# Frequency-domain mixing by three real products instead of four, an fp32 first transform stage, and a 512-wide weight conversion

## Chip, cores and metric

The kernel runs on one core of a Trainium2 chip, in one launch. The metric is device time in microseconds (us), the median of the runs shown. The engines are TensorE (PE, with its weight loads as PEld), VectorE (DVE), ScalarE (ACT), GpSimd (POOL) and SyncE (SP), which issues most DMAs.

## Reference

Three layers follow each other; `x` is 8 x 3072 x 256 in fp32.

```python
X = np.fft.rfft(x, axis=1); Xr, Xi = X.real, X.imag
Yr = Xr @ w_r - Xi @ w_i + b_r                 # mixing of channels, 256 x 256
Yi = Xr @ w_i + Xi @ w_r + b_i
Yr, Yi = soft_threshold(Yr, 0.01), soft_threshold(Yi, 0.01)
x = np.fft.irfft(Yr + 1j * Yi, n=3072, axis=1).reshape(24576, 256)
# soft mixture of experts over 8 batches of 3072 tokens, with an online softmax in the kernel
# gated feed-forward: rms norm, silu(xn @ w_gate) * (xn @ w_val) @ w_out    (weights in float64)
```

## The kernel before

The kernel has two phases. Phase 1 (`phase1`) does the transform, the mixing, the threshold and the sums of the softmax over tokens. Phase 2 does the feed-forward from what phase 1 kept; it takes some 1,095 us, and of it the change touches one line (917), which names three buffers.

**Precision.** TensorE multiplies either fp32 tiles or tiles of the type `fp32r`, which carry fewer bits. Where more bits are wanted from `fp32r`, a value is split into a high part (a copy rounded by ScalarE) and a low part (the rest, a subtraction), and products of parts are added up in PSUM. The trace shows an fp32 product as two records, each with its own weight load, and an `fp32r` product as one.

**Stages of phase 1, per batch.** The transform of length 3072 is split into 96 x 32.
- Stage A (`emit_A`, line 230) is a 96 x 96 product over pieces of 512 columns; a batch has 16 pieces, `g`. `split_hi` (208) and `split_lo` (224) make the two parts of the input, and line 245 does three `fp32r` matmuls. ScalarE evacuates (248), and the result goes to a DRAM buffer `bounce` and back in another order (`load_B`, 254).
- Stage B (`emit_B`, 261) is four fp32 matmuls of 128 x 128 (270). ScalarE writes the high part of the spectrum (277), VectorE the low part (280).
- Mixing (`emit_M`, 292) works on a window: a third of a batch, 512 columns, two halves `h` of the input channels and two halves `ch` of the output channels. There are 24 windows of 12 steps. Each of the four outputs (real or imaginary, `ch`) takes three steps of four `fp32r` matmuls (313): 48 a window. Then ScalarE (320) and VectorE (323) apply the threshold, both from PSUM.
- `emit_T` (353) transposes the result, `emit_L` (365) makes logits' spectra, and `chain` (384) is the list of the softmax work of one batch, by step.

**Order.** The schedule is by hand. The loop at line 693 runs the 288 steps `u`; a step emits for each engine, in program order: what `post` put off to this step (evacuations one step after their matmuls, VectorE's part two steps after), then chain work, `emit_M`, stage A, transposes, stage B. Each engine works its own list in order. PSUM banks: one for A, two for B, two for M, one for T.

**Weight conversion.** `converter` (100) turns the float64 weights into fp32 by integer operations on VectorE, 256 values wide: 36 jobs, nine or ten VectorE instructions each (132 to 150). It is a generator; line 743 lets it go on by one piece in those steps for which `load`, a running estimate of VectorE's work (tables `fixed` and `chained`, `pace` a step), is below `room`.

**Memory and the end of phase 1.** Pools are closed when their stage is done, and `Mid.open(n)` puts buffers of 1 MB in their place and loads expert weights into them (line 794, on SP): 5 buffers with 4 loads at step 252, 1 at step 279, 6 after the last step, 4 later. Behind these loads on SP stand the softmax result of the last batch (480), the four loads of `cs` (871) and what phase 2 starts with.

Of the kernel before, what the change touches and what calls it, by code (L numbers as in the profile page):

```python
# [99 lines left out]
def converter(tc, st, w_gate, w_val, w_out, wgv_d, wo_d):  # L100
# [4 lines left out]
    for i, w in enumerate((w_gate, w_val)):  # L105
        v = w.bitcast(I32).rearrange("(k p) f -> p k f", p=128)
        for k in range(2):
            for f in range(6):
                jobs.append((v[:, k, 512 * f:512 * f + 512], wgv_d[:, k, 1536 * i + 256 * f:1536 * i + 256 * f + 256]))
    v = w_out.bitcast(I32).rearrange("(k p) c -> p k c", p=128)  # L110
    for k in range(12):
        jobs.append((v[:, k, :], (wo_d[0][:, k, :], wo_d[1][:, k, :])))

    def load(n):
        t = raw_p.tile([128, 256, 2], I32, name="cvraw")
        nc.sync.dma_start(out=t.rearrange("p n w -> p (n w)"), in_=jobs[n][0])
        return t

    def steps():
# [3 lines left out]
        for n, (_, dst) in enumerate(jobs):  # L123
# [18 lines left out]
            w = tmp_p.tile([128, 256], F32, name="cvw")  # L142
            v.scalar_tensor_tensor(out=w, in0=q, scalar=2.0 ** -44, in1=m.bitcast(F32), op0=ALU.mult, op1=ALU.add)
            v.tensor_tensor(out=w, in0=w, in1=p.bitcast(F32), op=ALU.mult)
            if isinstance(dst, tuple):
# [3 lines left out]
                nc.sync.dma_start(out=dst[0], in_=h)  # L149
                v.tensor_tensor(out=w, in0=w, in1=h, op=ALU.subtract)  # L150
# [7 lines left out]
def phase1(tc, x, w_r, w_i, b_r, b_i, phi, t_d, t_bf, t_ci, t_ai, t_af, t_id,  # L158
# [24 lines left out]
    dh = ca.tile([96, 96], F32R, name="dh")  # L183
    dl = ca.tile([96, 96], F32R, name="dl")
    wh = {k: cm.tile([128, 2, 256], F32R, name=f"wh_{k}") for k in ("r", "n", "i")}
    wl = {k: cm.tile([128, 2, 256], F32R, name=f"wl_{k}") for k in ("r", "n", "i")}
# [5 lines left out]
    xraw, xsp, asb, bounce, bin_t, xq, x0, yy, yts, lfs, mns, mix = ({} for _ in range(12))  # L192
# [15 lines left out]
    def split_hi(g, dve=False):  # L208
        b, i, h = g // 16, g // 2 % 8, g % 2
        if b == 0 and i % 2:  # L210

            if h == 0:
                xsp["t"] = xq_p.tile([128, 2, 2, 2, 512], F32R, name="xq")[0:96]
            xs = xsp["t"][:, h, 0, 0, :], xsp["t"][:, h, 1, 0, :]
        else:
            xs = xs_p.tile([96, 512], F32R, name="xhi"), xs_p.tile([96, 512], F32R, name="xlo")
        v = xraw[b, i][:, 512 * h:512 * h + 512]
        if dve:
            nc.vector.tensor_copy(out=xs[0], in_=v)
        else:  # L220
            nc.scalar.activation(out=xs[0], in_=v, func=AF.Copy)  # L221
        xsp[g] = xs + (v,)

    def split_lo(g, eng):
        hi, lo, v = xsp[g]
        eng.tensor_tensor(out=lo, in0=v, in1=hi.bitcast(F32), op=ALU.subtract)  # L226
        if g % 2 and 8 <= g // 2 < 8 * NB - 2:
            load_x(*divmod(g // 2 + 2, 8))

    def emit_A(g, ps=None):  # L230
        b, i, h = g // 16, g // 2 % 8, g % 2
        hi, lo, _ = xsp.pop(g)
# [11 lines left out]
        for k, (w, v) in enumerate(((dh, hi), (dh, lo), (dl, hi))):  # L244
            nc.tensor.matmul(out=ps, lhsT=w, rhs=v, start=(k == 0), stop=(k == 2))  # L245
# [15 lines left out]
    def emit_B(b, q, h):  # L261

        t = bin_t[b, q]
        if h == 0 and q % 2 == 0:
# [957 lines left out]
```

## Time and profile before

| | |
|---|---|
| device time, three runs | 1793.46, 1796.31, 1796.82 us; median 1796.31 us |
| profiled execution: span from first to last instruction | 1798.8 us (no other time is recorded for it) |
| TensorE busy | 1767.3 us, 98% |
| VectorE, ScalarE, GpSimd busy | 1274.8, 1084.6, 242.1 us |
| steps 0 to 287 of phase 1, about | 47 to 630 us |

The page gives the busy time of each engine and what its idle time waited for. Matmuls are pipelined, so the length of one record is more than the time between two; the distance of starts in a dense run, or the pieces of the chain, give the time that one takes. All granted clocks here are those of TensorE.

### The profile page before, as it was taken

How to read it: one execution, taken by the hardware profiler on the slowest of the kernel's cores; microseconds unless marked ns; L12 is line 12 of the kernel's file. 1: busy time of each engine (PE TensorE's matmuls, PEld its weight loads, DVE VectorE, ACT ScalarE, POOL GpSimd, SP SyncE). 2: the span in 40 equal slices, each digit the busy share in tenths (PEclk: the TensorE clock that was granted, in tenths of full speed). 3: DMA queues.
4: the chain of work that ended last, by engine and by line, in shares of the span. 5: the costliest groups of instructions: out<-in, count | busy, mean ns of one | idle time of the engine just before them, and what ended most of it. 6: DMA issues, size and time to landing. Idle time of an engine off the chain costs nothing.

```text
span 1798.8 us, 33265 instructions
## 1 busy us (share of the span) xinstructions
PE 1767.3 (98%) x12910; PEld 1536.9 (85%) x12910; DVE 1274.8 (71%) x2126; ACT 1084.6 (60%) x2185; POOL 242.1 (13%) x181
## 2 busy tenths in 40 slices
PE   7999999999999989999999999999999999999999
PEld 5777777777777746999999999999999999999998
DVE  4478787785854537777677777777777777777775
ACT  3555556565553337776676676676676676676553
POOL 2434233332321001000000000000000000000000
PEclk8999999999999999999999999999999999999999
DMA  8865654756545197223123113212213203202101
GB/s 223 238 195 170 171 166 141 202 149 180 162 115 176 39 309 202 55 60 68 33 57 62 42 43 64 53 37 59 60 33 63 66 23 73 66 18 60 31 18 36
DMA packets 157101, 180.70 MB, mean 100 GB/s; under 512 B 62304, under 2 KB 126320, under 8 KB 156944
## 3 DMA queue, kind: packets, MB, share of 16 engines
q1 hardware_dynamic: 156208, 176.62, 37.4%
q8 instruction: 102, 1.67, 0.4%
q0 software_dynamic: 624, 1.92, 0.3%
q14 instruction: 55, 0.45, 0.1%
q10 hardware_dynamic: 112, 0.04, 0.0%
HBM read 94.36 MB, written 60.56 MB: 86 GB/s over the span
## 4 chain that ended last, share of the span: by engine, by line
PE 69%; DVE 1%; DMA 1%; SPq 1%; ACT 0%; issue 0%; POOL 0%; DVEq 0%
PE pe L1108 23%; PE po L1108 22%; PE pv L1072 7%; PE pg L1070 7%; PE psM L313 4%; PE psx L847 1%; PE psB L270 1%; DMA cs<-ct_d 1%; PE psA L245 0%; PE psT L361 0%; PE psT L373 0%; PE psC L552 0%; PE psC L396 0%; PE psx L1108 0%; SPq L854 0%; DMA cq<-ex 0%
## 5 line engine op out<-in xcount | busy, mean ns | idle before, releaser
L1076 DVE TENSOR_TENSOR h<-s,pv 128x512 f32<-128x512 f32 x576 | 394.2, 684 | 262.7 <-ACT s L1074 261.0
L1074 ACT ACTIVATE s<-pg 128x512 f32<-128x512 f32 x576 | 344.4, 598 | 346.5 <-PE pg L1070 344.5
L1108 PE MATMUL pe<-wo,hh 128*128 128x256 f32 x2304 | 429.0, 279 | 0.0
L1108 PE MATMUL po<-wo,hh 128*128 128x256 f32 x2280 | 423.6, 279 | 0.0
L1108 PEld LDWEIGHTS pe<-wo,hh 128*128 128x128 f32 x2304 | 382.6, 188 | 43.2 <-DVE o L1124 2.4
L97 DVE TENSOR_TENSOR hl<-h,hh 128x512 fp32r<-128x512 f32 x572 | 407.3, 712 | 0.0
L96 ACT ACTIVATE hh<-h 128x512 fp32r<-128x512 f32 x576 | 359.8, 625 | 8.0 <-DVE h L1076 6.9
L1108 PEld LDWEIGHTS po<-wo,hh 128*128 128x128 f32 x2280 | 349.8, 188 | 3.3
L1108 PE MATMUL pe<-wo,hl 128*128 128x256 f32 x1152 | 321.1, 279 | 0.0
L1108 PE MATMUL po<-wo,hl 128*128 128x256 f32 x1140 | 317.6, 279 | 0.0
L1070 PE MATMUL pg<-cq,gst 128*128 128x512 f32 x576 | 229.4, 398 | 0.3 <-ACT s L1074 0.3
L1072 PE MATMUL pv<-cq,gst 128*128 128x512 f32 x576 | 227.8, 395 | 0.7 <-DVE h L1076 0.7
L1108 PEld LDWEIGHTS pe<-wo,hl 128*128 128x128 f32 x1152 | 216.1, 188 | 0.0
L1108 PEld LDWEIGHTS po<-wo,hl 128*128 128x128 f32 x1140 | 213.9, 188 | 0.0
L226 POOL TENSOR_TENSOR xlo<-xraw,xhi 96x512 fp32r<-96x512 f32 x107 | 142.4, 1335 | 295.2 <-ACT xhi L221 195.1
L313 PE MATMUL psM<-xq,wh_r 128*128 128x512 f32 x384 | 174.3, 454 | 2.0 <-DVE xq L280 1.1
L277 ACT ACTIVATE xq<-psB 128x512 fp32r<-128x512 f32 x96 | 57.2, 596 | 120.4 <-PE psB L270 120.4
L280 DVE TENSOR_TENSOR xq<-psB,xq 128x512 fp32r<-128x512 f32 x96 | 66.0, 688 | 87.3 <-ACT xq L277 87.2
L270 PE MATMUL psB<-bf,bin 128*128 128x128 f32 x768 | 106.1, 282 | 7.6 <-DMA bin<-bounce 7.5
L270 PEld LDWEIGHTS psB<-bf,bin 128*128 128x128 f32 x768 | 95.8, 195 | 18.9 <-issue 16.5
L1072 PEld LDWEIGHTS pv<-cq,gst 128*128 128x128 f32 x576 | 108.3, 188 | 2.2 <-DVE h L1076 1.8
L1070 PEld LDWEIGHTS pg<-cq,gst 128*128 128x128 f32 x576 | 108.1, 188 | 1.3 <-ACT s L1074 1.1
(288 smaller groups left out, 2245.8 us busy)
## 6 DMA issues: line engine op xcount, KB each, us to landing
bin<-bounce SPq DMA_DIRECT2D x192, 128.0 KB, 3.7
bounce<-asb SPq DMA_DIRECT2D x59, 384.0 KB, 3.5
xraw<-in_x_dram SPq DMA_DIRECT2D x56, 384.0 KB, 4.2
ex<-in_moe_w_dram SPq DMA_DIRECT2D x16, 1024.0 KB, 12.2
out_dram<-o SPq DMA_DIRECT2D x124, 128.0 KB, 2.2
out_dram<-o SPq DMA_DIRECT2D x132, 64.0 KB, 1.7
cs<-chi SPq DMA_DIRECT2D x56, 96.0 KB, 2.1
cs<-clo SPq DMA_DIRECT2D x56, 96.0 KB, 2.2
```

The costliest lines, as they stand in the source:

```text
L96: nc.scalar.activation(out=hi, in_=src, func=AF.Copy)
L97: (lo_eng or nc.vector).tensor_tensor(out=lo, in0=src, in1=hi.bitcast(F32), op=ALU.subtract)
L226: eng.tensor_tensor(out=lo, in0=v, in1=hi.bitcast(F32), op=ALU.subtract)
L270: nc.tensor.matmul(out=ps[:, 128 * j:128 * j + 128], lhsT=t[:, j, 128 * h:128 * h + 128], rhs=bf[:, 4 * q + j, :], start=True, stop=True)
L277: nc.scalar.activation(out=hi, in_=v, func=AF.Copy)
L280: nc.vector.tensor_tensor(out=lo, in0=v, in1=hi.bitcast(F32), op=ALU.subtract)
L313: nc.tensor.matmul(out=ps, lhsT=w, rhs=v, start=(m % 3 == 0 and n == 0), stop=(m % 3 == 2 and n == 3))
L1070: nc.tensor.matmul(out=pg, lhsT=gst[:, 128 * fb:128 * fb + 128], rhs=v, start=True, stop=True)
L1072: nc.tensor.matmul(out=pv, lhsT=gst[:, 1536 + 128 * fb:1536 + 128 * fb + 128], rhs=v, start=True, stop=True)
L1074: nc.scalar.activation(out=s, in_=pg, func=AF.Silu)
L1076: nc.vector.tensor_tensor(out=h, in0=s, in1=pv, op=ALU.mult)
L1108: nc.tensor.matmul(out=ps, lhsT=a[:, ts], rhs=w[:, fb, :], start=(fb == 0 and k == 0), stop=(fb == 11 and k == 2))
```

## The change

Mixing uses Yr = w_r (Xr + Xi) - (w_i + w_r) Xi and Yi = w_r (Xr + Xi) + (w_i - w_r) Xr. The sum Xr + Xi is made in fp32 (a copy on ScalarE, an addition on VectorE) and its product is taken in fp32; the other two are taken from split halves with three `fp32r` matmuls each. The product with w_r is copied out of PSUM by ScalarE, VectorE adds it to each of the other two, and the threshold then works in SBUF. Stage A takes its input as it is, in one fp32 matmul. The conversion is 512 wide: 18 jobs in smaller pieces. The step tables, some steps of transposes, the buffers of phase 1 and the numbers given to `Mid.open` change with it.

```diff
@@ converter: jobs of 512, 18 instead of 36
-            for f in range(6):
+            for f in range(3):
...
-    for k in range(12):
-        jobs.append((v[:, k, :], (wo_d[0][:, k, :], wo_d[1][:, k, :])))
+    for k in range(0, 12, 2):
+        jobs.append((v[:, k:k + 2, :], tuple(w[:, k:k + 2, :].rearrange("p k c -> p (k c)") for w in wo_d)))
...
@@ pools of phase 1
-    xq_p, x0_p = P(st_m, "xq", 2), P(st_m, "x0", 2)
+    xq_p, xs_p, x0_p, s_p, r_p = (P(st_m, n, k) for n, k in (("xq", 2), ("xs", 1), ("x0", 2), ("s", 2), ("r", 1)))
...
-    xr_p, xs_p, as_p = P(st_a, "xr", 2), P(st_a, "xs", 4), P(st_a, "as", 2)
+    xr_p, as_p = P(st_a, "xr", 3), P(st_a, "as", 2)
...
-    def split_hi(g, dve=False):
...
-    def split_lo(g, eng):
...
@@ emit_A
-        for k, (w, v) in enumerate(((dh, hi), (dh, lo), (dl, hi))):
-            nc.tensor.matmul(out=ps, lhsT=w, rhs=v, start=(k == 0), stop=(k == 2))
+        nc.tensor.matmul(out=ps, lhsT=dt, rhs=xraw[b, i][:, 512 * h:512 * h + 512], start=True, stop=True)
+        if h == 1:
+            xraw.pop((b, i))
+            if 8 <= g // 2 + 3 < 8 * NB and g // 2 >= 8:
+                post(lambda: load_x(*divmod(g // 2 + 3, 8)))
...
@@ emit_B
         def evac():
             nc.scalar.activation(out=hi, in_=v, func=AF.Copy)
+            nc.scalar.activation(out=xsum, in_=v[:, 2:4], func=AF.Copy)
 
         def rest():
+            nc.vector.tensor_tensor(out=xsum, in0=v[:, 0:2], in1=xsum, op=ALU.add)
             nc.vector.tensor_tensor(out=lo, in0=v, in1=hi.bitcast(F32), op=ALU.subtract)
...
@@ emit_M
-        ri, ch = UNITS[m // 3]
+        (ch, k), h = ((0, 0), (1, 0), (0, 1), (0, 2), (1, 1), (1, 2))[m // 2], m % 2
...
+        if k == 0:
+            nc.tensor.matmul(out=ps, lhsT=wf[:, h, cs], rhs=xs[b, qq][:, h], start=(h == 0), stop=(h == 1))
         else:
-            terms = [(wh[key][:, h, cs], X[:, 1, h, part]) for h in range(2) for key, part in ways]
...
+            terms = ((wh, 0), (wl, 0), (wh, 1))
+            for n, (w, p) in enumerate(terms):
+                nc.tensor.matmul(out=ps, lhsT=w[k - 1][:, h, cs], rhs=X[:, p, h, k - 1], start=(h == 0 and n == 0), stop=(h == 1 and n == 2))
+        if h == 0:
             return
         o = 1 if qq == 0 else 0
-        Y = yy[b, qq][:, ri, ch, o:]
+        if k == 0:
+            t = mix["s", ch] = s_p.tile([128, 512], F32, name="s")
+            post(lambda: nc.scalar.activation(out=t[:, o:], in_=ps[:, o:], func=AF.Copy), 1, 0)
+            return
+        ri = 2 - k
+        Y, t, late = yy[b, qq][:, ri, ch, o:], mix["s", ch], int(m == 9)
+        r = r_p.tile([128, 512], F32, name="r")
+
+        def whole():
+            nc.vector.tensor_tensor(out=Y, in0=ps[:, o:], in1=t[:, o:], op=ALU.add)
 
         def first():
-            nc.scalar.activation(out=Y, in_=ps[:, o:512], func=AF.Relu, bias=b_lo[:, ri, ch:ch + 1])
+            nc.scalar.activation(out=r[:, o:], in_=Y, func=AF.Relu, bias=b_lo[:, ri, ch:ch + 1])
 
         def end():
-            nc.vector.scalar_tensor_tensor(out=Y, in0=ps[:, o:512], scalar=b_hi[:, ri, ch:ch + 1], in1=Y, op0=ALU.add, op1=ALU.min)
+            nc.vector.scalar_tensor_tensor(out=Y, in0=Y, scalar=b_hi[:, ri, ch:ch + 1], in1=r[:, o:], op0=ALU.add, op1=ALU.min)
...
-        post(first, 1, 0)
-        post(end, 2, 0)
+        post(whole, 1 + late, 0)
+        post(first, 2 + late, 0)
+        post(end, 3 + late, 0)
...
@@ the loop of steps
-    fixed = (0.7, 0.7, 0.0, 0.0, 1.15, 0.7, 0.0, 1.4, 0.0, 0.0, 1.4, 0.0)
+    fixed = (1.8, 0.75, 0.75, 0.0, 0.0, 1.55, 0.7, 1.1, 1.45, 0.0, 1.85, 0.7)
...
-    load, room, pace = 0.0, 0.4, 1.75
+    load, room, pace = 0.0, 1.0, 1.85
...
-        if w >= 1 and m in (1, 5, 8, 10) and w <= W - 3:
+        if w >= 1 and m in (2, 5, 8, 10) and w <= W - 3:
...
-            mid.open(5, 4)
+            mid.open(4, 3)
...
-    mid.open(6)
+    mid.open(7)
```

Before the first step, `split_x` and the splits of `w_r` and `w_i` (each high and low, and the negated pair on line 620) go; instead the two matrices w_i - w_r and -(w_i + w_r) are made on VectorE and split, and w_r is loaded into `wf` as it is. A third tile of the next batch's input is loaded there, behind the third `load_B`. The 96 x 96 table is loaded into `dt` and not split.

## Rows read from the trace of the kernel before

**Rows 1.** Page, busy time, share and instructions of each engine.
```profile
PE 1767.3 (98%) x12910; PEld 1536.9 (85%) x12910; DVE 1274.8 (71%) x2126; ACT 1084.6 (60%) x2185; POOL 242.1 (13%) x181
```
**Rows 2.** Windows: length, busy us (instructions) of PE, PEld, DVE, ACT, POOL, clock, DMA share, GB/s.
```profile
0.00:47.00 47.00, 35.48 (x131) 26.01 (x132) 20.52 (x36) 18.16 (x32) 14.72 (x17) 0.85 0.82 214
...
265.00:338.00 73.00, 72.69 (x506) 55.40 (x508) 58.74 (x106) 41.29 (x75) 25.68 (x19) 1.00 0.60 168
...
47.00:630.00 583.00, 577.25 (x4084) 437.36 (x4083) 399.60 (x694) 306.33 (x555) 176.43 (x135) 0.99 0.57 162
```
**Rows 3.** Waits of PE, 120 to 484 us: total us, times, longest us (the first row).
```profile
PE psM L313 <- DVE xq L280: 1.1, 1, 1.1
```
**Rows 4.** Chain of waits, 600 to 632 us: start us, us, what.
```profile
603.21 2.80 PE psM L313 x12
...
609.65 0.86 PE psC L503 x2
610.51 0.93 PE psM L313 x4
```
**Rows 5.** Timeline of PE in the first step: start us, us, instruction.
```profile
47.69 0.39 PE L245 MATMUL psA<-xhi,dh 96*96 96x512 f32 x1
...
48.38 0.40 PE L313 MATMUL psM<-xq,wh_r 128*128 128x512 f32 x1
```
**Rows 6.** Groups by line, all of the span: VectorE and ScalarE, 512 and 256 wide.
```profile
L97 DVE TENSOR_TENSOR hl<-h,hh 128x512 fp32r<-128x512 f32 x572 | 407.3, 712 | 0.0
L1076 DVE TENSOR_TENSOR h<-s,pv 128x512 f32<-128x512 f32 x576 | 394.2, 684 | 262.7 <-ACT s L1074 261.0 <-PE pv L1072 0.6
...
L1044 ACT ACTIVATE sq<-psx 128x256 f32<-128x256 f32 x168 | 62.3, 381 | 0.0
L277 ACT ACTIVATE xq<-psB 128x512 fp32r<-128x512 f32 x96 | 57.2, 596 | 120.4 <-PE psB L270 120.4
...
L1124 DVE COPY o<-pe 128x256 f32<-128x256 f32 x96 | 36.0, 416 | 4.7 <-PE pe L1108 4.7
```
**Rows 7.** The same view: costliest and cheapest of the conversion's nine lines of 36.
```profile
L144 DVE TENSOR_TENSOR cvw<-cvw,cva 128x256 f32<-128x256 f32 x36 | 31.8, 882 | 1.2
...
L138 DVE TENSOR_SCALAR cve<-cvraw 128x256 int32<-128x256 int32 x36 | 12.4, 345 | 0.0
```
**Rows 8.** By source line, two conversion lines: ns min/median/max, first and last start.
```profile
L132 DVE TENSOR_SCALAR cva<-cvraw x36: 225/293/1234, 71.8 to 488.7; 128x256 int32<-128x256 int32 x36
...
L144 DVE TENSOR_TENSOR cvw<-cvw,cva x36: 424/427/1402, 76.7 to 497.2; 128x256 f32<-128x256 f32 x36
```
**Rows 9.** Groups by line, GpSimd, 47 to 630 us.
```profile
L226 POOL TENSOR_TENSOR xlo<-xraw,xhi 96x512 fp32r<-96x512 f32 x105 | 139.9, 1336 | 281.1 <-ACT xhi L221 181.0 <-PE psA L245 52.9 <-ACT yy L320 22.4
L464 POOL TENSOR_TENSOR ch<-ch,mc 96x1024 f32<-96x1024 f32 x7 | 13.7, 1957 | 7.0 <-ACT xq L277 7.0
```
**Rows 10.** Timeline of all engines before the first step.
```profile
6.00 0.44 PE L245 MATMUL psA<-xhi,dh 96*96 96x512 f32 x1 [0.49 <-DVE xhi L219]
...
22.41 0.47 PE L245 MATMUL psB<-xq,dh 96*96 96x512 f32 x1 [0.97 <-POOL xq L226]
...
32.21 0.42 DVE L620 TENSOR_SCALAR wl_n<-wl_i 128x512 fp32r<-128x512 f32 x1
...
32.86 3.42 PE L270 MATMUL psB<-bf,bin 128*128 128x128 f32 x16 [3.00 <-DMA bin<-bounce]
```
**Rows 11.** Timeline of SP's DMA issues, end of phase 1.
```profile
611.63 45.74 SPq L794 DMA_DIRECT2D ex<-in_moe_w_dram  x12
657.46 3.39 SPq L480 DMA_DIRECT2D c_d<-ch  x1
```
**Rows 12.** Chain of waits, 628 to 705 us.
```profile
662.36 13.17 DMA cs<-ct_d
```
**Rows 13.** Windows, one of the stretch after the last step, columns as in rows 2.
```profile
640.00:648.00 8.00, 6.76 (x87) 3.73 (x89) 7.52 (x15) 5.18 (x9) 0.00 (x0) 1.00 1.09 351
```

More of the change, by code (lines that the diff above doesn't have):

```diff
@@ L182, in phase1 @@
     ph = cinv.tile([128, 2, 32], F32, name="ph")
[L183 to L186, printed above, removed]
+    dt = ca.tile([96, 96], F32, name="dt")
+    wh = [cm.tile([128, 2, 256], F32R, name=f"wh{k}") for k in range(2)]
+    wl = [cm.tile([128, 2, 256], F32R, name=f"wl{k}") for k in range(2)]
     wf = cm.tile([128, 2, 256], F32, name="wf")
@@ L190, in phase1 @@
     b_hi = cm.tile([128, 2, 2], F32, name="b_hi")
-    xraw, xsp, asb, bounce, bin_t, xq, x0, yy, yts, lfs, mns, mix = ({} for _ in range(12))
+    xraw, asb, bounce, bin_t, xq, xs, x0, yy, yts, lfs, mns, mix = ({} for _ in range(12))
     pend, clock = {}, [None]
@@ L265, in emit_B @@
             xq[b, q // 2] = xq_p.tile([128, 2, 2, 2, 512], F32R, name="xq")
+            xs[b, q // 2] = xs_p.tile([128, 2, 512], F32, name="xs")
         if h == 0 and q == 0:
@@ L312, in emit_M @@
-        for n, (w, v) in enumerate(terms):
-            nc.tensor.matmul(out=ps, lhsT=w, rhs=v, start=(m % 3 == 0 and n == 0), stop=(m % 3 == 2 and n == 3))
-        if m % 3 < 2:
+        if k == 0:
+            nc.tensor.matmul(out=ps, lhsT=wf[:, h, cs], rhs=xs[b, qq][:, h], start=(h == 0), stop=(h == 1))
+        else:
+            X = xq[b, qq]
+            terms = ((wh, 0), (wl, 0), (wh, 1))
+            for n, (w, p) in enumerate(terms):
+                nc.tensor.matmul(out=ps, lhsT=w[k - 1][:, h, cs], rhs=X[:, p, h, k - 1], start=(h == 0 and n == 0), stop=(h == 1 and n == 2))
@@ L354, in emit_T @@
         Y = yy[b, q // 2]
-        if ri == 0:
+        if (b, q) not in yts:
             yts[b, q] = yt_p.tile([128, 4, 256], F32, name="yt")
@@ L593, in chain @@
                 lambda: mid.slots(bank(psM, "psM"))]
-    raw = ch_p.tile([128, 1024], F32, name="ch")
-    nc.scalar.dma_start(out=raw[0:96, 0:96], in_=t_d)
+    nc.scalar.dma_start(out=dt, in_=t_d)
     for i in range(8):
@@ L609, in phase1 @@
     warm_up(5)
-    split(nc, raw[0:96, 0:96], dh, dl)
     for k, w in enumerate((b_r, b_i)):
@@ L616, in prep_w @@
         flat = lambda t: t.rearrange("p k m -> p (k m)")
-        for key, src in (("r", rw[:, 0:512]), ("i", rw[:, 512:1024])):
-            split(nc, src, flat(wh[key]), flat(wl[key]))
-        for w in (wh, wl):
-            nc.vector.tensor_scalar(out=flat(w["n"]), in0=flat(w["i"]).bitcast(F32), scalar1=-1.0, scalar2=None, op0=ALU.mult)
-        nc.gpsimd.tensor_copy(out=flat(wf), in_=rw[:, 0:512])
+        wr, wi, t = flat(wf), rw[:, 0:512], rw[:, 512:1024]
+        for k in range(2):
+            if k == 0:
+                nc.vector.tensor_tensor(out=t, in0=wi, in1=wr, op=ALU.subtract)
+            else:
+                nc.vector.scalar_tensor_tensor(out=t, in0=wi, scalar=-1.0, in1=wr, op0=ALU.mult, op1=ALU.subtract)
+            split(nc, t, flat(wh[k]), flat(wl[k]))
         nc.vector.tensor_scalar(out=b_lo, in0=bias, scalar1=-LAM, scalar2=None, op0=ALU.add)
@@ L634, in phase1 @@
     banks = [(psA, "psA"), (psM, "psM"), (psB, "psB"), (psT, "psT"), (psB, "psB"), (psM, "psM")]
-    def split_x(g):
-        split_hi(g, g % 4 != 3)
-        split_lo(g, nc.gpsimd if g % 8 in (1, 4, 6) else nc.vector)
-    GA, AHEAD = 17, 5
-    for g in range(AHEAD):
-        split_x(g)
+    GA = 17
     for g in range(16):
@@ L659, in phase1 @@
     load_B(0, 2)
+    load_x(1, 2)
     for c in range(-6, 0):
```

80 lines of the change are left out of this document (23 added, 57 removed).

## Prediction

> **What bounds the kernel now.** I read the busy line of the page first: TensorE is busy for 98% of the span, VectorE for 71%, ScalarE for 60% [rows 1]. A mean over stages says little, so the windows come next. Three stretches matter: up to 47 us, before the first step, PE is busy for 35.5 us only and the DMA share is 0.82; from 47 to 630 us, the 288 steps, PE is busy for 577.25 of 583 us at a granted clock of 0.99, with VectorE at 399.6, ScalarE at 306.3 and GpSimd at 176.4 us [rows 2]; behind that lie 75 us of latency and DMA, and then phase 2, which the change does not touch but for the names of buffers. Third, the waits of PE: the longest that it had in 364 us of steps is 1.1 us [rows 3]. So in the steps PE's own stream sets the pace, and what is taken out of it comes off the time, as long as the other engines keep up. VectorE is the nearest to the limit: in a stretch with conversion it is busy for 58.7 of 73 us, 80% [rows 2].
>
> **The price of a matmul.** The chain gives it without overlap: twelve `fp32r` matmuls of 512 columns take 2.80 us, 0.233 us each, and one fp32 matmul of 512 columns (two records, 96 input rows, as in stage A) takes 0.86 us [rows 4]. Stage A's three `fp32r` matmuls begin at 47.69 and PE's next work begins at 48.38, 0.69 us for three [rows 5].
>
> **Mixing.** A window has 48 `fp32r` matmuls. After, each of the six units is two steps: two units of two fp32 matmuls and four of six `fp32r`. So 24 `fp32r` go and 4 fp32 come: -24 x 0.233 + 4 x 0.86 = -5.59 + 3.44 = -2.15 us a window, -51.6 us over 24 windows.
>
> **Stage A.** 0.86 in place of 0.69 us is +0.17 us a piece. 128 pieces less the 17 before the steps are 111: +18.9 us. All of it is on PE's stream. Together the steps' stream is shorter by 32.7 us, 1.36 us a window: 24.3 becomes 22.9 us.
>
> A rule of the Trainium skill speaks against this change: "FP8 and Floating Point Precision", section TensorE Precision Notes, says that a true fp32 product goes through the array in four passes. By it and the 0.233 us of a single pass an fp32 matmul would be 0.93 us, mixing would save 44.7 and stage A cost 26.9 us. The row with 0.86 us is the nearer witness and I keep it: two records with two weight loads carry less overhead than four.
>
> **VectorE.** The steps' 399.6 us change so. The conversion's nine lines of 36, from 12.4 to 31.8 us, and 12 instructions of line 150 (7.8 us) sum to 175 us [rows 7]; their medians, 0.293 us (L132) and 0.427 us (L144), are far below their means and their longest are 1.2 and 1.4 us [rows 8], because they lose time beside GpSimd's 105 subtractions of 1.34 us [rows 9], which the change takes away. At the medians the 175 us would be 114; twice as wide and half as many they lie between 114 (no gain from width) and 87 (0.42 us for a 512-wide single-input operation [rows 10], 0.70 for one with two inputs [rows 6], 18 jobs of six and three, and 6 x 0.70). I take 95, near the 512-wide rows. Added: 96 sums of 256 columns at 0.42 us (nearest row L1124, same width from PSUM), 40 us; 96 `whole` at 0.684 (L1076, PSUM and SBUF), 66 us [rows 6]. `end` stays at 0.7 us. The few subtractions of stage A on VectorE, 3 us, go. Sum: 400 - 175 + 95 + 40 + 66 - 3 = 423 us in some 550: 77%, and about 88% while the conversion runs. It fits, with little air.
>
> **ScalarE and GpSimd.** ScalarE loses 109 copies of 0.62 us and gains 96 of 0.38 (L1044) and 48 of 0.60 (L277): 306 - 68 + 37 + 29 = 304 us [rows 2, 6]; no effect. GpSimd keeps the chain's work.
>
> **Hand-offs in PSUM.** Here new waits can come. `emit_M` has two banks; a unit was three steps and is now two, and a bank is free only when VectorE has done `whole`. Behind a late `whole` ScalarE stands in `first`, and behind that its evacuations. The narrow place is the window's start. Stage B of step 10 ends as step 11 begins. ScalarE then copies for 0.60 + 0.38 us, VectorE needs 0.42 + 0.69 for the sum and the low part and 0.69 for the `whole` of the last unit: 2.8 us. PE reaches step 2, which needs that bank, after step 11 (0.70 + 0.86) and the lone fp32 matmuls of steps 0 and 1 (1.72): 3.3 us. The slack is 0.5 us, the sum itself is needed a step earlier, and a piece of conversion put at step 10 (two 512-wide instructions, up to 1.4 us) exceeds it by up to 0.9 us. No row shows this wait. Bounds: 0, and 0.9 us in each of 24 windows, 22 us. Worked through with `fixed` and `pace`, the conversion still runs from step 12 to about step 218, as now, and has a piece at step 10 in two windows of three, some 12 of them; I take +5 us. A gain beyond the stream is bounded by PE's idle time in the stage, 5.75 us [rows 2]; I count none.
>
> **Before the first step.** Stage A's 16 pieces there begin at 6.00 us behind a split and wait for parts (0.97 us for GpSimd at 22.41), and the first stage B waits at 32.86 us for DMA that follows the last evacuation [rows 10]. Sixteen fp32 matmuls need 13.8 us; from about 5.5 us they end at 19.3, against 23.7 now, if the input comes in time and the clock is full; at a granted 0.85 for this stretch [rows 2] they end later. Bounds -4.5 and 0; I take -2.5 us. The matrices for the mixing are made on VectorE and ScalarE beside that DMA wait. The third input tile is issued after the last `load_B`, so nothing on SP stands behind it that PE is waiting for.
>
> **After the last step.** The early expert load that no longer fits at step 252 goes to the end: 7 loads after the last step. There SP is the path: twelve loads of 1 MB occupy its queue from 611.63 to 657.36 us, behind them it waits for the softmax result and then issues `cs`, whose 13.17 us the chain holds [rows 11, 12]. The DMAs move 351 GB/s there [rows 13], so 1 MB more is 3.0 us, all of it on the path. Bounds 0 (if that queue has time to spare) and 4; I take +3.0 us. The last threshold gains a link, `whole`, 0.7 us, which these loads cover.
>
> **Sum.** -51.6 + 18.9 + 5 - 2.5 + 3 = -27.2 us, from a span of 1798.8 to 1771.6 us. The median of the runs shown is 2.5 us below that span, so I state 1796.3 - 27.2 = 1769 us.
>
> **Rivals.**
> - *VectorE becomes the bound during the conversion.* If its instructions keep their dear mean, 175 us over 17 windows is 10.2 us a window; the rest is (400 - 175 - 3 + 106)/24 = 13.7: 23.9 us against PE's 22.9. Then 17 windows gain 1.0 us less, +17 on top: 1786 us. For: 88% and work in order. Against: the subtractions that made it dear go. Chance 0.13.
> - "SBUF — State Buffer", section Who interferes with whom, in the Trainium skill, gives one shared port pair to VectorE and GpSimd, locked for a whole instruction; by it `end`, now with both inputs in SBUF, can stand behind the chain's GpSimd work too. Its 1.96 us each (L464) [rows 9], 16 of them, are 31 us at most on VectorE, and inside this rival.
> - *An fp32 matmul costs four single passes among the others,* 0.93 us. Then mixing gives -1.86 us a window and stage A costs +0.24 a piece: -44.7 + 26.9 + 5.5 = -12.3, 1784 us. For: only isolated pairs are in the rows. Against: rows 4. Chance 0.05.
> - *The window's start stalls every time.* PE finds the bank of step 2 taken in each window because ScalarE and VectorE begin late and a piece of conversion stands before them; the exposed time is the full 2.8 us. From (51.6 - 18.9 + 2.5 - 3)/24 = 1.34 us a window on the kernel is slower. At 2.8 us: -32.2 + 67 = +35, 1831 us. For: the 0.5 us of slack. Against: the low share of VectorE in the windows without conversion. Chance 0.08.
> - *What is won in the steps is lost around them* (input tiles late in the first window, the tail's DMA): within 0.2%, 1796 us. Chance 0.05.
> - The forecast, 0.69.
>
> **Numbers.** A measurement of this kernel tells changes of about 0.2%, 3.6 us, from none. Faster: 0.69 + 0.13 + 0.05 = 0.87, of which 0.01 goes to each of the others: 0.85. Same 0.06, slower 0.09. The forecast's own range is -32.7 - 4.5 + 0 - 5.75 (PE's idle gone too) to -32.7 + 0 + 22 + 4, 1753 to 1790. The likely part of it with the first two rivals is 1756 to 1787, which leaves out the stalled start, the null case and the ends: about 0.2.
>
> **What would show it.** In the steps, PE busy to 98% over about 550 us (545 to 560), an fp32 matmul of the mixing and of stage A at 0.86 us in the chain, and PE's waits for `whole` or for the sum at 10 us or less in all. VectorE at 400 to 440 us there, conversion near 95 us. The steps begin 2 to 3 us earlier, and the stretch from the last step to phase 2 is 3 us longer, with thirteen loads before `cs`. The prediction is wrong if PE waits more than 1.3 us a window on VectorE's `whole` or the sum, or if fp32 matmuls stand at 0.93 us or more.

## The result and the profile after

The changed kernel takes 1781.43 us (median of 4 runs, 1778.69 to 1783.5) against 1796.57 us before on the same chip: a ratio of 0.9916 [0.99, 0.9931], 15.1 us less. A second measurement beside four other kernels gave 0.993 [0.9915, 0.9944], 1782.43 us. The forecast was 1769 us, 27 us less, with a range of 1756 to 1787: the direction held, and 12 of the 27 us are missing.

The page's busy line after, then two windows (columns as in [rows 2]), before the first step and the 288 steps:
```profile
PE 1737.3 (98%) x12398; PEld 1443.0 (81%) x12398; DVE 1267.7 (71%) x2122; ACT 1073.4 (60%) x2206; POOL 102.1 (6%) x67
```
```profile
0.00:46.60 46.60, 33.26 (x111) 20.64 (x112) 6.45 (x16) 14.69 (x26) 6.89 (x15) 0.93 1.00 272
46.60:603.30 556.70, 545.47 (x3592) 346.90 (x3591) 405.31 (x708) 298.13 (x581) 44.29 (x22) 1.00 0.57 163
```
In the steps PE is still busy for 98%, over 556.7 us, as foretold. VectorE needs 405 us (forecast 423), ScalarE 298 (304). Ahead of the first step PE is at a higher clock and less busy than in [rows 2], but the DMA share is now 1.00. PE's waits in the steps (total us, times, longest) are few:
```profile
PE psT L356 <- DVE lf L371: 3.4, 4, 1.0
PE psT L356 <- ACT yt L358: 2.1, 4, 0.7
PE psM L297 <- DVE yy L310: 1.9, 1, 1.9
PE psB L254 <- DMA bin<-bounce: 1.3, 1, 1.3
PE psM L297 <- ACT s L303: 0.8, 1, 0.8
PE psC L410 <- ACT ch L411: 0.7, 1, 0.7
```
(After's lines: stage A L224, stage B L254, mixing L292 in fp32 and L297 in `fp32r`, sum L267, low part L268, `s` L303, `whole` L310, `first` L313, `end` L316, T L356, L L368, `csub` L459, bounce write L233, expert loads L766.)

I cut every trace at the first weight load of the mixing in each window, the last one of all, and the first weight load of the gated feed-forward in phase 2 ("first up" in the expectations). In us; "to phase 2" runs from the last step; the rows below the changed kernel are the runs of the next section:

| kernel | first step at | windows 0-3 | 4-17 | 18-20 | 21 | 22-23 | steps | to phase 2 | phase 2 |
|---|---|---|---|---|---|---|---|---|---|
| before | 46.6 | 96.0 | 357.7 | 71.4 | 22.0 | 36.2 | 583.2 | 62.8 | 1106.2 |
| before, again | 44.2 | 94.4 | 355.0 | 71.4 | 22.0 | 36.2 | 579.1 | 61.8 | 1107.8 |
| after | 46.6 | 89.3 | 341.9 | 67.6 | 20.9 | 37.0 | 556.7 | 66.8 | 1108.4 |
| after, again | 45.7 | 89.4 | 343.8 | 67.6 | 20.9 | 35.9 | 557.6 | 68.1 | 1108.4 |
| stage A alone | 45.7 | 96.7 | 361.7 | 72.8 | 22.0 | 36.2 | 589.4 | 60.9 | 1107.1 |
| no conversion | 47.3 | 89.3 | 336.2 | 67.6 | 20.9 | 37.0 | 551.0 | 66.5 | 1107.2 |
| one load fewer | 46.5 | 89.4 | 342.9 | 67.6 | 20.9 | 37.0 | 557.7 | 65.5 | 1107.9 |
| bias tiles moved | 48.3 | 88.7 | 341.7 | 67.6 | 20.9 | 35.8 | 554.6 | 65.3 | 1106.3 |
| late softmax | 47.5 | 88.9 | 341.9 | 67.6 | 20.9 | 34.0 | 553.3 | 68.1 | 1105.4 |
| other order at start | 44.9 | 89.6 | 341.9 | 67.6 | 20.9 | 37.0 | 557.0 | 67.1 | 1107.3 |
| conversion kept out | 45.3 | 89.1 | 344.7 | 70.8 | 26.4 | 37.4 | 568.5 | 68.4 | 1105.0 |
| conversion 256 wide | 45.1 | 88.8 | 345.7 | 71.2 | 29.5 | 35.9 | 571.1 | 66.1 | 1108.3 |
| all three | 45.3 | 89.4 | 342.7 | 67.5 | 20.9 | 34.0 | 554.6 | 64.4 | 1109.0 |
| all three, two `r` | 43.2 | 89.0 | 339.6 | 67.6 | 20.9 | 32.9 | 549.9 | 64.8 | 1106.6 |

By the means of two profiles each, the steps gave 24.0 us (581.1 to 557.1), the stretch behind them took back 5.2 (62.3 to 67.5), the others 0.7 and 1.4: 16.7 in sum, near the medians' 15.1. Windows that have nothing irregular agree to 0.05 us between profiles; the first step's time and phase 2 scatter by 1 to 3 us with unchanged code, so the 0.7 and the 1.4 are within that scatter.

### The profile page after: what moved, and what is told of

Its sections match the earlier page's. It is cut to its first block, busy times and chain, and to the rows that moved or that the text cites. A ratio compares the mean times of both kernels' runs of the same rounds, so it can differ in the third digit from the quotient of the medians.

```text
span 1778.4 us, 32004 instructions
## 1 busy us (share of the span) xinstructions
PE 1737.3 (98%) x12398; PEld 1443.0 (81%) x12398; DVE 1267.7 (71%) x2122; ACT 1073.4 (60%) x2206; POOL 102.1 (6%) x67
## 4 chain that ended last, share of the span: by engine, by line
PE 87%; DVE 5%; DMA 4%; ACT 3%; issue 1%; SPq 0%; POOL 0%; ACTq 0%
PE pe L1080 23%; PE po L1080 23%; PE pg L1042 8%; PE pv L1044 8%; PE psM L297 5%; PE psB L254 4%; PE psA L224 4%; PE psM L292 3%; PE psT L356 2%; PE psx L819 1%; PE psT L368 1%; PE psC L547 1%; DMA bin<-bounce 1%; DMA bounce<-asb 1%; ACT r L313 1%
## 5 line engine op out<-in xcount | busy, mean ns | idle before, releaser
L297 PE MATMUL psM<-xq,wh 128*128 128x512 f32 x384 | 179.9, 478 | 2.7 <-DVE yy L310 1.9
L254 PEld LDWEIGHTS psB<-bf,bin 128*128 128x128 f32 x768 | 97.9, 196 | 25.7 <-issue 21.4
L267 DVE TENSOR_TENSOR xs<-psB,xs 128x256 f32<-128x256 f32 x96 | 40.5, 422 | 105.6 <-ACT xs L264 105.4
L254 PE MATMUL psB<-bf,bin 128*128 128x128 f32 x768 | 104.1, 280 | 10.9 <-DMA bin<-bounce 9.7
L224 PE MATMUL psA<-xraw,dt 96*96 96x512 f32 x212 | 108.8, 594 | 0.6
```

The lines of the kernel that those rows point to most:

```text
L224: nc.tensor.matmul(out=ps, lhsT=dt, rhs=xraw[b, i][:, 512 * h:512 * h + 512], start=True, stop=True)
L254: nc.tensor.matmul(out=ps[:, 128 * j:128 * j + 128], lhsT=t[:, j, 128 * h:128 * h + 128], rhs=bf[:, 4 * q + j, :], start=True, stop=True)
L297: nc.tensor.matmul(out=ps, lhsT=w[k - 1][:, h, cs], rhs=X[:, p, h, k - 1], start=(h == 0 and n == 0), stop=(h == 1 and n == 2))
```

## The experiments

**The two kernels again.** No edit.

> The kernel before, unchanged, for a second profile of it. Theory: the 5 us by which the two profiled executions differ more than the medians do (20.4 us of span against 15.1 us) are the spread of single executions, so this span lies between 1790 and 1799 us, the 288 steps (first product of the mixing to the last) again take 583.3 us within 1 us and the stretch from the last step to the first h of phase 2 64.8 us within 1 us. Rival: the first profile of before was typical and the steps really take longer or shorter by several us from run to run, then the steps' length differs by over 2 us.

Span 1792.8 us; first step 2.5 us earlier, steps 4.2 us shorter than in the first profile, all of it in windows 0 to 17: over 2 us, the sign that the rival had named. Measured to the first `h` (the first product of the feed-forward's two halves) the last stretch was 63.8 us. The first profile of before was thus a long execution, and the 20.4 us between the first two spans overstate the gain; the scatter lies in the steps too.

> The changed kernel, unchanged, on the chip of the three runs beside it, so that they can be set against it. Theory: 14 to 16 us below the kernel before, and the profile's stretches as in the first one: steps 555 to 558 us, window 22 between 19 and 21 us, first step at 45.3 to 48.3 us, last step to first up matmul 65.3 to 68.1 us. Rival (the profiles of the changed kernel seen so far are a biased few): steps or either end outside these.

12.6 us below before, just under the theory's range; all stretches inside. Window 22 took 19.3 us against 20.7.

**Stage A alone.**
```diff
-        for k, (w, v) in enumerate(((dh, hi), (dh, lo), (dl, hi))):
-            nc.tensor.matmul(out=ps, lhsT=w, rhs=v, start=(k == 0), stop=(k == 2))
+        nc.tensor.matmul(out=ps, lhsT=dt, rhs=xraw[b, i][:, 512 * h:512 * h + 512], start=True, stop=True)
```
in the kernel before, with `split_hi` and `split_lo` gone.

> The kernel before with only stage A changed: one fp32 matmul of 0.86 us in the place of three fp32r ones, the splits of x gone, three x buffers. Theory of the forecast: +0.17 us for each of the 111 pieces in the steps, +18.9 us, nothing before the first step and nothing after the last: steps 602 us against 583.3, total 1815 us (1812 to 1818). Rival 1: the splits' work on ScalarE, VectorE and GpSimd had been holding the steps up, so its removal gives part of it back: under +14 us. Rival 2: an fp32 matmul costs four passes of 0.233 us there: over +24 us.

1805.04 against 1795.85 us, 1.005 [1.0037, 1.0063]: +9.2 us, half of the forecast; rival 1. The piece did cost what was forecast where nothing else changes: windows 8, 11 and 14, with five pieces and no lost time before, grew from 25.99 to 26.93 us, 0.19 each. The other half came back with the splits' work, which left three engines. The steps of before (second profile) and of this kernel, then the conversion's L144 in either (ns min/median/max):
```profile
44.20:623.20 579.00, 574.15 (x4086) 436.00 (x4085) 400.33 (x694) 305.87 (x555) 176.89 (x136) 1.00 0.57 163
```
```profile
45.60:635.10 589.50, 588.54 (x3976) 419.12 (x3976) 342.76 (x689) 257.05 (x446) 36.00 (x22) 1.00 0.56 156
```
```profile
L144 DVE TENSOR_TENSOR cvw<-cvw,cva x36: 424/426/1403, 76.9 to 490.6; 128x256 f32<-128x256 f32 x36
```
```profile
L144 DVE TENSOR_TENSOR cvw<-cvw,cva x36: 424/425/426, 72.8 to 500.8; 128x256 f32<-128x256 f32 x36
```
VectorE lost 57.6 us of busy time with five instructions fewer: with GpSimd's subtractions gone, no L144 takes longer than 0.426 us. ScalarE lost 48.8 us. PE, which had 4.85 us of idle time, has 1.0. In before (second profile) its longest waits in the steps were for VectorE and for ScalarE's evacuation of stage A (248); the second line is one in each of the windows 3, 6, 9, 12, 15 and 18, shown for window 6 in PE's timeline below it:
```profile
PE psM L313 <- DVE xq L280: 1.2, 1, 1.2
PE psA L245 <- ACT asb L248: 1.1, 6, 0.2
PE psC L245 <- ACT asb L248: 1.0, 1, 1.0
```
```profile
190.84 0.39 PE L313 MATMUL psM<-xq,wl_n 128*128 128x512 f32 x1
191.42 0.47 PE L245 MATMUL psA<-xhi,dh 96*96 96x512 f32 x1 [0.19 <-ACT asb L248]
```
Those six windows grew by 0.56 us for six pieces, half of the price. So VectorE's relief is not the whole of it; how much came from each engine was not tried apart. The timeline also shows that the idle time of the view is less than what a wait costs: 0.58 us from start to start, where 0.23 is usual, with 0.19 of it counted as idle.

**The conversion's arithmetic left out**: of each piece's lines only the load and the stores stay.
```diff
-            v.tensor_tensor(out=w, in0=w, in1=p.bitcast(F32), op=ALU.mult)
```
and the eight before it alike.

> The changed kernel with the arithmetic of the weight conversion left out (the raw pieces are still loaded, and zeros are stored for the converted weights, so phase 2 computes with zeros); VectorE loses about 95 us of work in the steps. Theory: the steps are bound by PE, and all the conversion costs there are late hand-offs: steps 553.5 to 556.7 us against 556.7 in the changed kernel. Rival (VectorE bounds the windows with conversion): steps at most 547 us.

Steps 551.0 us in its one execution: -5.7, between the two. All of it is in the middle window of each batch: 4, 7, 10, 13 and 16 go from 22.7-23.9 to 22.1-22.5 us, the windows 3, 5, 6, 8, 9 and so on don't move by 0.03. So the conversion is hidden in two windows of three, and costs about 1.1 us in those where the chain of the batch has VectorE too. Of PE's waits for T (L340, L342 here) only these are left:
```profile
PE psT L340 <- ACT yt L342: 1.0, 3, 0.5
```
The 3.4 us for `lf` are gone and 1.1 of 2.1 us for `yt`: 4.5 of the 5.7 us are T finding its one bank not yet emptied.

**One expert load fewer** after the last step.
```diff
+            if skip and k == 0:
+                src, tiles, *_ = self.todo.pop(0)
+                tiles.append(tiles[-1])
+                continue
             self.load(-1)
```

> The changed kernel with the first of the seven expert loads after the last step left out (one expert computes with its neighbour's first-layer weights). Theory (the term of the tail): each 1 MB load there is on the path for 3.0 us; the stretch from the last step to the first h of phase 2 goes from 70.7 to 67.2 to 68.2 us, the total by -3 us to about 1778. Rival: the stretch is set by when the loads may begin (they wait for the last end) and by the chain of the last batch, and a load more or less is hidden: under 1 us.

1778.27 us, 0.9896 [0.988, 0.9911], 3.6 and 6.1 us less than after's two ratios give. The stretch was 65.5 us against 66.8 and 68.1; to the first h, as the expectation counts, 67.4 against 68.8 and 70.1 (its 70.7 was read further on). So the load is worth 2.0 us there by the mean of after's two profiles (1.3 to 2.7 by either), not 3.0.

**Bias tiles out of the way of that load.**
```diff
-    bias = cm.tile([128, 2, 2], F32, name="bias")
+    bias = cst.tile([128, 2, 2], F32, name="bias")
```
and `b_lo`, `b_hi` alike.

> The changed kernel with its three bias tiles moved out of the memory that the first of the seven expert loads takes over, so that this load needn't wait for the last end (which reads b_hi). Theory (beside the extra 1 MB, the tail lost 2 to 3 us because the loads begin 3.2 us after the last step instead of at once): the first load is issued within 0.5 us of the last step and the stretch from there to the first up matmul of phase 2 goes from 66.8 to 64 to 65 us, the total by -2 to -3 us. Rival (the transfers are not the end of that stretch all the way, as leaving out a whole load brought only 1.4 us of 3.0): under 1 us.

0.9905 [0.989, 0.992]. SP's issues after the last step, of after (its last step at 603.25) and of this kernel (602.83):
```profile
606.89 29.28 SPq L766 DMA_DIRECT2D ex<-in_moe_w_dram  x12
636.27 3.29 SPq L475 DMA_DIRECT2D c_d<-ch  x1
```
```profile
603.53 29.08 SPq L766 DMA_DIRECT2D ex<-in_moe_w_dram  x12
632.70 3.86 SPq L475 DMA_DIRECT2D c_d<-ch  x1
```
The first load starts 0.7 us behind the last step in the place of 3.6, and the stretch is 65.3 us, 2.2 below the mean of after's two and just above the 64 to 65 expected. Only this one load is freed: the second still waits for the last `end` (316), by the waits of SP's queue, of after and of this kernel, and begins 3.6 us behind the last step.
```profile
SPq L766 <- DVE ex L316: 20.0, 1, 20.0
```
```profile
SPq L766 <- DVE ex L316: 2.5, 1, 2.5
```
This run and the next two had no changed kernel beside them, and the intervals of their ratios overlap with after's; what each gained is read from its windows.

**The column softmax of batch 6 in window 23.**
```diff
-                    (12, L(dmax, 0, 32)), (13, L(dpar, 32)), (14, cmax), (15, csub), (18, L(dmn, 32)), (18, L(dsub, 0, 32)),
-                    (19, L(dexp, 0, 32)), (19, alexp), (20, cexp), (21, csum), (22, cmul), (22, L(fa, 0, 16), 1),
+                    (12, L(dmax, 0, 32)), (13, L(dpar, 32)), *c_at[:2], (18, L(dmn, 32)), (18, L(dsub, 0, 32)),
+                    (19, L(dexp, 0, 32)), (19, alexp), *c_at[2:], (22, L(fa, 0, 16), 1),
```
with steps 26, 27, 29, 31, 32 in `c_at` for that batch.

> The changed kernel with the column softmax of batch 6 (cmax, csub, cexp, csum, cmul) moved by 12 to 10 steps, from window 22 into window 23, where VectorE is busy for 9.5 of 16.5 us. Theory: in window 22 VectorE (18.7 of 20.7 us busy, an end of 2.04 us beside csub) is what holds PE and so lets the granted clock fall; then window 22 goes from 20.7 to 16 to 18 us, window 23 gains at most 0.5, the total by -2.5 to -4.5 us. Rival (the narrow place is the single r buffer and the order of the hand-offs in a window without transposes and pieces of stage A, whatever VectorE's load): window 22 stays over 19.5 us.

0.9901 [0.9883, 0.9919]; window 22 took 17.7 us, window 23 the same 16.3: the theory. What went on in window 22 of after, by VectorE's and PE's timelines:
```profile
576.11 2.06 DVE L442 TENSOR_TENSOR ch<-ch,mn 96x1024 f32<-96x1024 f32 x1
578.01 0.41 DVE L267 TENSOR_TENSOR xs<-psB,xs 128x256 f32<-128x256 f32 x1
578.34 0.68 DVE L268 TENSOR_TENSOR xq<-psB,xq 128x512 fp32r<-128x512 f32 x1
578.93 2.04 DVE L316 SCALAR_TENSOR_TENSOR yy<-yy,b_hi,r 128x512 f32<-128x512 f32 x1
580.90 0.68 DVE L310 TENSOR_TENSOR yy<-psM,s 128x512 f32<-128x512 f32 x1
```
```profile
581.63 0.50 PE L297 MATMUL psM<-xq,wh 128*128 128x512 f32 x1 [1.90 <-DVE yy L310]
...
584.29 1.69 PE L498 MATMUL psC<-ch,af 96*128 96x512 f32 x2
```
and of GpSimd:
```profile
578.03 2.39 POOL L459 TENSOR_TENSOR ch<-ch,mc 96x1024 f32<-96x1024 f32 x1 [6.74 <-ACT r L313]
```
One `end` takes 2.04 us beside `csub`, the next `whole` stands behind it, and PE waits 1.90 us for that. Here the granted clock then falls. Windows of after's first profile and of this kernel, window 22 and the stretch behind the wait:
```profile
566.30:586.90 20.60, 17.79 (x85) 11.70 (x84) 18.61 (x28) 10.90 (x21) 5.40 (x3) 0.92 0.02 7
...
582.60:585.90 3.30, 3.30 (x12) 2.44 (x11) 3.23 (x9) 1.77 (x5) 2.17 (x1) 0.54 0.00 0
```
```profile
566.80:584.50 17.70, 16.19 (x85) 10.52 (x84) 14.15 (x23) 9.53 (x20) 0.84 (x1) 1.00 0.04 5
```
VectorE's 18.6 of 20.6 us become 14.2 of 17.7. In after's second profile `end` took 2.02 us and PE waited the same 1.9, but the clock stayed at 1.00, and window 22 cost 1.4 us less:
```profile
567.40:586.70 19.30, 16.49 (x86) 10.54 (x85) 17.50 (x26) 10.26 (x20) 5.18 (x3) 1.00 0.01 1
```
Seven profiles have that 1.9 us wait in window 22, after's two and those of five runs that leave this window alone: four took 20.7 us there with the fall of the clock, three 19.3 us without it. So the move gains 1.5 us where the clock stays, and the fall, where it comes, costs another 1.4.

**Another order before the first step.**
```diff
-            elif b == 0 and i >= 6:
+            elif b == 0 and i >= 5:
...
     load_x(1, 0)
-    load_x(1, 1)
     prep_w()
     load_bf(1, nc.sync)
     load_B(0, 1)
+    load_x(1, 1)
```

> The changed kernel with two things altered before the first step: piece 10 of stage A goes into a buffer of its own, so that its eviction no longer waits 6.6 us for a write to DRAM, and the load of the second x block is moved behind the stage-B load of q = 1. Theory 1 (the eviction's wait delays the last writes and all behind them): the first step begins at 43.5 to 45 us against 46.6, the total -2 to -3 us. Theory 2 (the transfers fill the time before the first step, DMA share 0.99, so an earlier write only waits elsewhere): only the moved 384 KB count, at the 250 GB/s of that stretch 1.5 us, so 45 to 46 us. Rival: the first step waits for the mixing weights or stage A's next piece, nothing changes.

0.9907 [0.989, 0.9924]. First step at 44.9 us, and 45.3 and 43.2 in the two versions below; in the eight profiles with the order of after it was at 45.1 to 48.3, mean 46.5. So 2.1 us on average, which fits either theory (ScalarE's wait of 6.6 us for the bounce write is gone, the DMA share is still 0.99); the two edits were not tried apart.

**The conversion kept out of steps 13 to 19 of each batch.**
```diff
-        if load < room and (u == 0 or u > 10):
+        if load < room and (u == 0 or u > 10) and (u < 40 or not 13 <= u % 36 < 20):
```

> The changed kernel with no step of the weight conversion in steps 13 to 19 of each batch's 36 (from window 4 on), where the chain's maxima and csub lie; the conversion ends in window 20 or at the start of window 21 instead of window 18. Theory (the conversion cost 5.7 us of the steps, all of it in the windows 4, 7, 10, 13, 16, by 1.1 us each): these windows go from 23.4 to 22.1 to 22.6 us, the steps by -3 to -5 us, and window 19 doesn't grow by more than 0.5. Rival (what costs is the conversion's sum of work, 19 ns of PE wait for each 100 ns of it, wherever it lies): the steps within 1.5 us of 556.7.

A miss: 0.9979 [0.9968, 0.9989], steps 568.5 us. Windows 13 and 16 fell to 22.1 and 22.4 us as the theory wants, but 4, 7 and 10 stayed (23.4, 23.7, 23.8), and 17, 19 and 21 grew by 3.8, 2.5 and 5.5: PE now waited 2.1 and 4.4 us for `bin`; SP, which issues those loads in order among the conversion's loads and stores, itself waited up to 20.8 us at a time for ScalarE's copy of a piece. Where the middle windows' time goes is only half shown.

**The conversion 256 wide again**, `converter` as in the kernel before.
```diff
-            p = tmp_p.tile([128, 512], I32, name="cva")
+            p = tmp_p.tile([128, 256], I32, name="cva")
```

> The changed kernel with the weight conversion as before, 256 wide (24 pieces of it, all else changed). Its VectorE work was 96 us in the changed kernel at 512 wide, and 123 us at 256 wide beside a stage A without splits. Theory: 26 us more of VectorE work and twice the steps cost at the 5.7 us per 96 us of the changed kernel another 1.5 us, and at most 6 if the windows 4, 7, 10, 13, 16 are already full: total +1 to +6 us against the changed kernel. Rival (the wide pieces are what makes the mixing's hand-offs late, since one holds VectorE for 0.7 us in the place of 0.4): 1 to 4 us faster.

0.9998 [0.9987, 1.0009], 12.3 us slower than after beside it, twice what the theory allowed. Of that 8.6 us are window 21 and 2.8 window 19. PE's longest wait there, and that window:
```profile
PE psB L250 <- DMA bin<-bounce: 5.3, 1, 5.3
```
```profile
550.80:580.30 29.50, 23.31 (x158) 15.82 (x157) 13.09 (x25) 10.87 (x24) 0.00 (x0) 0.88 0.58 170
```
The planner's places run out: the rest is done in one go at step 252, SP reaches the three expert loads at 555.5 us, and the window's `bin` loads behind them come late (in after: 530.1 us). So it isn't a clean price of the width: in windows 0 to 17, where none of this acts, 256 wide costs 1 to 4 us. VectorE's conversion was 121.6 us against 95 to 96. The rival, a gain from narrower pieces, did not come.

**All that gained, together** (the diffs of the bias tiles, the late softmax and the order at the start), and then with `s` in Y's real half and two `r`:
```diff
-... (("xq", 2), ("xs", 1), ("x0", 2), ("s", 2), ("r", 1)))
+... (("xq", 2), ("xs", 1), ("x0", 2), ("r", 2)))
-            t = mix["s", ch] = s_p.tile([128, 512], F32, name="s")
+            t = mix["s", ch] = yy[b, qq][:, 0, ch]
```

> The changed kernel with the three alterations that each gained alone: bias tiles out of the way of the expert loads, batch 6's column softmax in window 23, the order before the first step. Theory (they lie in different stretches and add): -2 for the tail, -2.9 in window 22, -1.5 to -2 before the first step: -5 to -7 us against the changed kernel, a ratio to the kernel before of 0.987 to 0.989; first step at 45 us, window 22 at 17.7 us, tail 64.5 to 66 us. Rival (the ends only trade times with each other: an earlier end of the steps meets expert loads that are no earlier): under -4 us.

1772.61 us, 0.9876 [0.9859, 0.9893], 9.8 us below after beside it, more than the theory's 5 to 7. Between the two profiles it is 6.7 us: 3.0 in the steps, 3.8 behind them, 0.4 before, and 0.6 lost in phase 2; so the three add, within the scatter of 1 to 3 us that one profile has.

> The version combo with s kept in the yet unwritten real half of Y in the place of a tile of its own, and the memory used for a second r buffer. Theory (what is left of the mixing's missing gain are waits of first for the end before it, which put off ScalarE's copy of s, and with it PE: 0.8 us in window 22, and part of the 1.1 us in the windows with conversion): window 22 from 17.7 to 16 to 17 us, windows 4, 7, 10, 13, 16 by 0.2 to 0.8 us each, -2 to -5 us against combo. Rival (whole and end wait for VectorE itself, however many r there are): within 1 us of combo.

1769.21 us, 0.9853 [0.9837, 0.987]: 3.4 us below combo and 25.8 below the kernel before. Window 22 took 16.7 us, windows 4, 7, 10, 13 and 16 22.59, 22.94, 23.53, 22.95 and 22.74 (combo: 23.26, 24.50, 23.94, 23.46, 22.71). PE's waits in its steps:
```profile
PE psT L356 <- ACT yt L358: 3.7, 5, 1.1
PE psB L254 <- DMA bin<-bounce: 1.2, 1, 1.2
PE psC L410 <- ACT ch L411: 0.7, 1, 0.7
PE psM L297 <- DVE yy L310: 0.7, 1, 0.7
```
PE has no wait for `lf` or `s` left: part of the hand-off loss was the single `r`, as the theory says, as far as the move of `s`, made with it and not tried apart, is without effect.

## Why the prediction was right, and where it was not

**The bound and the price: right.** PE is the bound in the steps, and an fp32 matmul costs 0.86 us, in stage A as in the mixing: two records each, so "x6" below are three matmuls. PE's timeline after, ahead of the first step, and the chain:
```profile
5.49 1.02 PE L224 MATMUL psA<-yt,dt 96*96 96x512 f32 x2
6.35 1.02 PE L224 MATMUL psM<-yt,dt 96*96 96x512 f32 x2
...
20.64 1.07 PE L224 MATMUL psB<-yt,dt 96*96 96x512 f32 x2 [0.68 <-DMA yt<-in_x_dram]
```
```profile
587.54 2.58 PE psM L292 x6
```
Starts are 0.86 us apart, and 2.58/3 is 0.86. The four passes of the Trainium skill ("FP8 and Floating Point Precision", TensorE Precision Notes) at 0.233 us each would be 0.93; the measurement decides for 0.86.

**Mixing and stage A: near in sum, because two errors offset each other, which is luck.** By windows, forecast stream against what the means of two profiles show: 0 to 3, -4.0 and -5.9; 4 to 17, -17.5 and -13.5; 18 to 20, -4.75 and -3.8; 21, -2.15 and -1.1; 22 and 23, -4.3 and +0.25. Stage A alone cost 8.3 us (589.4 against a mean of 581.1) in place of 18.9. The failed step is "A gain beyond the stream is bounded by PE's idle time in the stage, 5.75 us [rows 2]; I count none": the relief of VectorE and ScalarE that I had worked out myself was priced at nothing on PE, and the bound was no bound, since 10.6 us came back where PE's idle time was 4.85 to 5.75 (a wait costs more than the view counts as idle).

The mixing, with the new conversion and tables, brought by difference from stage A alone 32.3 us (589.4 to 557.1) in place of 51.6 less 5. Window by window against stage A alone the price of 2.15 us was right, and the loss has a place: windows 0, 1, 5, 8, 11, 14 and 17 gained 2.13 to 2.17 us each. Windows 4, 7, 10, 13 and 16 together gained 1.0 us in place of 10.75, and window 22 became 1.9 us longer in place of 2.15 shorter. These six hold 13.8 of the 19.3 us that are missing against 51.6.

**Hand-offs: +5 us, and the wrong place.** PE waits for `whole` or the sum for 2 us in all by its list of waits, so neither the window's start nor step 10 is narrow. The loss lies in window 22, where no T and no stage A stand between the units and one `whole` stood behind a slow `end` (window 23, without them too, gained 1.65 us), in the middle windows, where leaving out the conversion gave 5.7 us back, and in links that had a step's time and now have less: in window 21 the second `ainv` waits 0.7 us for ScalarE's copy of the first, which it did not before. T and L, which share one bank, now follow each other in neighbouring steps too. Not all of the missing time is assigned, and no run did the mixing alone.

**VectorE: right, and for the reason given.** The conversion took 96 us (forecast 95), the sums 40.5. [rows 8] had shown that its dear mean came from instructions beside GpSimd; stage A alone shows it. The Trainium skill ("SBUF — State Buffer", Who interferes with whom) says that a VectorE instruction with two SBUF inputs and a GpSimd one that reads SBUF exclude each other; the trace agrees, with 426 ns against 1403 ns at most for L144, and with the `end` of 2.04 us, which has both inputs in SBUF since the change. The rival that VectorE becomes the bound fell: without the conversion's 96 us the steps were 5.7 us shorter, not 17. Its busy time was 405 us for 423 forecast, although the added terms came as forecast: part of the difference is that records which follow each other closely overlap (as VectorE's in window 22 do), which busy time counts once and the forecast's sum did not.

**Before the first step: wrong.** "From about 5.5 us they end at 19.3, ..., if the input comes in time": it doesn't. Stage A waits for `yt` from 14 us on and ends at 22.4 us; the first step is no earlier (0.7 us later, within the scatter) in place of 2.5 earlier. The forecast looked at the transfers on SP alone. GpSimd issues eight loads, 1.77 MB in all (`ci`, `ident`, `ph`, `ai`, `af`), whose place in the program is steps 6 to 32. In the kernel before, its subtractions and a copy of w_r stand ahead of them in its list; in the changed kernel nothing does, and they go out at 3.4 to 10.5 us, among the input tiles. GpSimd's timelines, before and after, and then of stage A alone, where the copy of w_r still stands ahead of them:
```profile
75.79 0.57 POOL L717 DMA_DIRECT2D ci<-in_t_ci_dram  x1
```
```profile
4.70 1.64 POOL L692 DMA_DIRECT2D ci<-in_t_ci_dram  x3
```
```profile
27.27 2.17 POOL L675 DMA_DIRECT2D ci<-in_t_ci_dram  x4
```
In stage A alone the same sixteen pieces end at 19.0 us, as forecast, and the first stage B begins 6.5 us earlier than in the changed kernel. PE's timelines, after and stage A alone, last piece and first stage B:
```profile
21.54 1.02 PE L224 MATMUL psT<-yt,dt 96*96 96x512 f32 x2
...
35.78 3.75 PE L254 MATMUL psB<-bf,bin 128*128 128x128 f32 x16 [7.17 <-DMA bin<-bounce]
```
```profile
18.12 1.02 PE L220 MATMUL psT<-yt,dt 96*96 96x512 f32 x2
...
29.31 3.76 PE L249 MATMUL psB<-bf,bin 128*128 128x128 f32 x16 [4.11 <-DMA bin<-bounce]
```
There the eight loads go out at 26 to 30 us instead, the third stage B waits 5.0 us for `bin`, and the first step is at 45.7 us all the same. By an estimate from the 272 GB/s of this stretch after, 1.77 MB are 6.5 us of transfers. No run held the loads back, so what they cost in all is not shown.

**After the last step: the term was too small.** Forecast +3.0, measured +5.2. The load itself is worth 2.0 us (one load fewer). The step that failed is "`whole`, 0.7 us, which these loads cover": the loads don't cover it, they wait for it. The first load's memory takes in `b_hi`, which the last `end` reads, and SP issues in order, so all loads start 3.6 us behind the last step; moving the bias tiles, 48 bytes a partition, let one load start at once and gave 2.2 us back. About 1 us of the 5.2 is not assigned. [rows 11] were also read too broadly: the first of the twelve loads there is that of step 279, the other eleven begin at 630.5 us, 0.7 us behind the last step.

**Sum.** -24.0 + 0.7 + 5.2 and 1.4 us of scatter in phase 2 against -27.7 - 2.5 + 3: 3.7 us missing in the steps, 3.2 before them, 2.2 behind. The last version shows that more was to be had: its steps are 31.2 us shorter than before's mean. That is near the stream's 32.7, but with stage A's cheaper price in it; against stage A alone it is 39.5 of 51.6.

## What to carry to other kernels

Cheaper work on the bound shortens the steps, and every chain that is laid out in steps gets less time: after such a change look for the links that stood one step apart, single buffers between engines (`r`), and memory that is reused one instruction later. When an instruction's mean is far above its median, look who runs beside it before pricing its removal: taking 100 subtractions off GpSimd gave VectorE 57 us. When an engine that issues transfers loses work, ask which of its transfers come forward and what they meet there: here 1.77 MB met the input, in a stretch that was short of DMA. And compare window by window, not in sum: a sum near the forecast hid two terms that were off by 10.6 and 14.3 us.

## What the runs showed of the hardware that I had not expected

- GpSimd is lengthened as well: `csub` took 2.0 us on average before [rows 9], 2.4 with stage A alone, and 3.0 and 2.5 in the two profiles after. Which of VectorE's instructions does it was not tried.
- After a wait of 1.9 us with PE lightly used around it (1.80 of 3.70 us busy), the granted clock was 0.54 for 3.3 us in after's first profile, 1.2 GHz for nearly all of it: one fp32 matmul (two records), 0.86 us elsewhere in the chain, took 1.49 us. Of seven profiles with the same wait four show such a fall (0.53 to 0.59 in that stretch) and three stay at 1.00, after's second profile among them; what parts them no run shows.
- Equal code before the first step began its steps between 45.1 and 48.3 us in eight profiles; differences of 2 us in this start, with a DMA share of 1.00, say nothing from one trace.
